# Attention feeding a soft mixture of experts: x transposed in its own cycle, logits and slot sums one pair sooner, one group left at the end

## The chip, the cores and the metric

The kernel runs on one core of a Trainium2 chip, as one program. The time is device microseconds of one execution; of several executions the median is given. A profile of one further execution gives the rows below.

## The reference, cut to what matters

Three stages follow each other: attention inside chunks of 64 positions, a soft mixture of experts over the resulting 4608 x 512 matrix `x`, and a gated feed-forward layer.

```python
# attention, B=8, H=8, S=576, D=64, chunks of 64
scores = scale * (q_c @ k_c.T); scores -= scores.max(-1)
attn = exp(scores); attn /= attn.sum(-1) + 1e-9
x = (attn @ v_c) -> 4608 x 512
# mixture: N=4608 tokens, 8 experts x 4 slots = 32 slots
logits = x @ phi
d = exp(logits - logits.max(0)); d /= d.sum(0) + 1e-9
slot_input = d.T @ x                       # 32 x 512
for e in range(8):                          # w1: 512 x 1024, w2: 1024 x 512
    slot_out[e] = relu(slot_input[e] @ w1[e]) @ w2[e]
c = softmax over the slots of logits
x = c @ slot_out
# gated layer, d_ff = 1536
out = (silu(x @ w_gate) * (x @ w_val)) @ w_out
```

The weights of the gated layer arrive as 64-bit floats and are turned into single precision on the chip; the experts' weights are single precision.

## The kernel before, in words

The order of the instructions on each engine is the order in which the code is written.

**The attention loop.** It takes 36 tiles of 128 tokens, two at a time: 18 pairs. Iteration `k` does, on TensorE (PE): for the pair `a = k - 1` the product with v (`emit_pv`, tiles `xa_ps`, `xb_ps`); then either the logits of a group of four tiles (`emit_logits`, `lt_ps`) or the slot sums of a group (`emit_si`, `si_ps`); then the transposes of the exponentials' input for pair `k` (`emit_pt`, `pt_ps`), the scores of pair `k + 1` (`emit_scores`, `s_ps`), the transposes of `x` (`emit_xt`, `xt_ps`), and after logits the transpose of their exponentials (`emit_et`, `e_ps`). The logits run over all tokens, so the maximum per slot is a running one, and `acc` (slot sums) and `zst` (denominators) are rescaled by `beta_t` group by group.

**Who evacuates.** VectorE (DVE) takes the scores' maximum and subtracts it (`m`, `ssb`, lines 336 and 338), makes `x` out of `xa_ps` and `xb_ps` (`rec`, `x_sb`, lines 381 to 388), the running maximum (`mx`, `mn`) and `acc`. ScalarE (ACT) takes the exponentials (`pt`, `et`), copies `xt` and keeps a copy of the logits in `lt_all`. The PSUM pool `ps_t` has three buffers that `lt`, `pt`, `xt`, `e`, `si` take in turn: the first `xt_ps` of an iteration with logits gets the buffer of `lt_ps`, and so waits for `lt_all` (line 453).

**Loads.** All come from the queue of SyncE (SP), in the order of the code. `load_qk` follows the scores of the tile that had the buffer (four buffers), `load_v` follows its product (four buffers). `pump(1)` at the end of an iteration takes the next load from a list `lq` into one of 16 slots of 1 MB (`wp`): pieces of w1 and w2 in the main. Iterations with `k % 4 == 3` take none, except that the sixteenth takes two. Behind the loop four more slots (`wx`) open in the memory of the q, k and v buffers; from there on a piece is requested when a slot is freed, and the first are freed by the first products with w1 (`emit_w1`, `h_ps`).

**Conversion steps on the side.** From `k = 4` on `conv_step` puts one step of a weight's conversion at an iteration's end: step a (lines 185 to 187) at `k` = 4 and 7, b (194, 195) at 5 and 8, c (200) at 6 and 9.

**The tail and the experts.** Behind the loop two groups of logits (7 and 8) and two of slot sums remain. Then `sips` (line 623) forms the slots' inputs, and the experts run: `emit_w1` for six experts, `emit_w2` for two, and so on by the list `order`. The gated layer follows.

Of the kernel before, what the change touches and what calls it, by code (L numbers as in the profile page):

```python
# [8 lines left out]
F32 = mybir.dt.float32  # L9
# [24 lines left out]
def tile_attn_softmoe_swiglu(  # L34
# [12 lines left out]
    nc = tc.nc  # L47
# [220 lines left out]
    with tc.manual_schedule():  # L268
# [126 lines left out]
        def emit_xt(i):  # L395
            xt = xtp.tile([128, 4, 128], F32, tag="xt", name="xt")
            n = 4 if i < NTILE - 1 else 2
            for j0 in range(0, 4, n):
                ps = ps_t.tile([128, 4, 128], F32, tag="t", name="xt_ps")
                for j in range(j0, j0 + n):  # L400
                    nc.tensor.transpose(ps[:, j - j0, :], x_t[i][:, j * 128:(j + 1) * 128], ident)  # L401
                if j0 == 0:
                    nc.scalar.activation(out=xt[:, 0:n], in_=ps[:, 0:n], func=ACTF.Copy)  # L403
                else:
                    nc.vector.tensor_copy(out=xt[:, j0:j0 + n], in_=ps[:, 0:n])
            xt_t[i] = xt
# [4 lines left out]
        lt_t = {}  # L411
        lx_t = {}

        def emit_lmm(g, lt=None):
            if lt is None:
                lt = ps_t.tile([128, 512], F32, tag="t", name="lt_ps")
            lt_t[g] = lt
            for kk in range(4):
                for jt in range(4):
                    nc.tensor.matmul(  # L420
                        out=lt[32 * jt:32 * jt + 32, 0:128],
                        lhsT=phi_sb[:, kk, :],
                        rhs=xt_t[4 * g + jt][:, kk, :],
                        start=(kk == 0), stop=(kk == 3),
                        tile_position=(0, 32 * jt),
                    )

        def emit_lmax(g):
            lt = lt_t[g]
            mx = sm.tile([128, 1], F32, tag="mx", name="mx")  # L430
            mn = sm.tile([128, 1], F32, tag="mn", name="mn")
            nc.vector.tensor_reduce(out=mx, in_=lt[:, 0:128], axis=AX.X, op=ALU.max)
            if g:
                nc.vector.tensor_scalar(out=mn, in0=mx, scalar1=mrun[0], scalar2=-1.0, op0=ALU.max, op1=ALU.mult)
            else:
                nc.vector.tensor_scalar(out=mn, in0=mx, scalar1=-1.0, scalar2=None, op0=ALU.mult)
            if g:
                nc.vector.tensor_tensor(out=mx, in0=mx, in1=mrun[0], op=ALU.max)
            lx_t[g] = mn, mrun[0]
            mrun[0] = mx  # L440
# [15 lines left out]
        def emit_logits(g):  # L456
            emit_lmm(g)
            emit_lmax(g)
            emit_lexp(g)
# [3 lines left out]
        def emit_et(g, sums=True):  # L463
            et, z = et_t[g]
            ps = ps_t.tile([128, 512], F32, tag="t", name="e_ps")
            nc.tensor.transpose(ps[:, 0:128], et, ident)
            e = atp.tile([128, 128], F32, tag="e", name="e", bufs=1)
            nc.scalar.activation(out=e, in_=ps[:, 0:128], func=ACTF.Copy)
            e_t[g] = e
            if sums:  # L470
                emit_zst(g)

        def emit_zst(g):
            z = et_t.pop(g)[1]
            if g:
                nc.vector.scalar_tensor_tensor(out=zst, in0=zst, scalar=beta_t[g], in1=z, op0=ALU.mult, op1=ALU.add)
            else:
                nc.vector.tensor_copy(out=zst, in_=z)

        def emit_si(g):  # L480
            e = e_t.pop(g)
            ps = ps_t.tile([128, 512], F32, tag="t", name="si_ps")
            for jt in range(4):
                nc.tensor.matmul(  # L484
                    out=ps[32 * jt:32 * jt + 32, :],
                    lhsT=e[:, 32 * jt:32 * jt + 32],
                    rhs=x_t.pop(4 * g + jt),
                    start=True, stop=True,
                    tile_position=(0, 32 * jt),
                )  # L490
            if g:
                be = beta_t.pop(g)
                n = DM // 2 if g == NG - 1 else DM
                for o in range(0, DM, n):
                    nc.vector.scalar_tensor_tensor(
                        out=acc[:, o:o + n], in0=acc[:, o:o + n], scalar=be, in1=ps[:, o:o + n],
                        op0=ALU.mult, op1=ALU.add,
                    )
            else:
                nc.vector.tensor_copy(out=acc, in_=ps)  # L500
# [3 lines left out]
        def emit_m1():  # L504
            mps = ps_t.tile([128, 512], F32, tag="t", name="mps")
            nc.tensor.transpose(mps[0:1, 0:128], mrun[0], ident)
            nmrow = sm.tile([1, 4, 32], F32, tag="nmrow", name="nmrow", bufs=1)
            nc.vector.tensor_reduce(
                out=nmrow[:, 0, :], in_=mps[0:1, 0:128].rearrange("p (j s) -> p s j", s=32), axis=AX.X, op=ALU.max,
                negate=True,  # L510
            )
            for jj in range(1, 4):
                nc.vector.tensor_copy(out=nmrow[:, jj, :], in_=nmrow[:, 0, :])
            tail['nmrow'] = nmrow

        def emit_m2():
# [28 lines left out]
        for k in range(NP + 1):  # L545
            a = k - 1
            if a >= 0:
                emit_pv(a)
            if k == NP:
                break  # L550
            if a >= 3 and a % 2:
                emit_logits((a - 3) // 2)
            elif a >= 4:
                emit_si((a - 4) // 2)
            emit_pt(2 * k)
            emit_pt(2 * k + 1)
            if k + 1 < NP:
                emit_scores(k + 1)
                spread_v(2 * k + 2)
                spread_v(2 * k + 3)  # L560
            if a >= 1:
                emit_xt(2 * a - 2)
                emit_xt(2 * a - 1)
            if a >= 3 and a % 2:
                emit_et((a - 3) // 2)
            if k == 0 or k % 4 != 3:
                pump(1)
            elif k + 1 == NP - 2:
                pump(2)
            conv_step(k >= 4 and conv_pos() < 2 and not conv_busy())  # L570
# [3 lines left out]
        auto[0] = True  # L574
        pump()
        g = NG - 1
        lt2 = ps_s.tile([128, 2, 512], F32, tag="s", name="lt_ps")
        emit_xt(NTILE - 4)
        emit_xt(NTILE - 3)
        emit_lmm(g - 1, lt2[:, 0])  # L580
        emit_xt(NTILE - 2)
        emit_lmax(g - 1)
        emit_xt(NTILE - 1)
        emit_lexp(g - 1)
        emit_lmm(g, lt2[:, 1])
        emit_et(g - 1, False)
        emit_lmax(g)
        emit_lexp(g)
        emit_zst(g - 1)
        emit_m1()  # L590
        emit_si(g - 1)
        emit_et(g, False)
        emit_m2()
        nc.scalar.activation(out=lt_all[:, g, :], in_=lt_t[g][:, 0:128], func=ACTF.Copy)
# [1 line left out]
        emit_zst(g)  # L596
        emit_si(g)
        conv_until(2)
        warm(3)
        p1.close()  # L600

        p2 = ctx.enter_context(tc.tile_pool(name="p2", bufs=1))
# [416 lines left out]
```

## Time and profile before

| what | value |
|---|---|
| median of 3 runs | 545.47 us (544.68 to 545.85) |
| the profiled execution's own time | 543.5 us |
| its span, first to last instruction | 541.7 us |
| mean granted TensorE clock | 0.996 of full speed |
| PE busy over the span | 521.3 us (96%) |
| DVE, ACT, POOL busy | 406.7, 260.4, 252.9 us |
| attention with its tail | to about 130 us |
| experts | about 131 to 169 us |
| gated layer | the rest |

The span is 1.8 us under the execution's time, and that time is 2.0 us under the median of the runs. Busy time of PE is not work at its peak: matmuls wait inside the pipeline too, and their ends are modelled.

### The profile page before, as it was taken

Reading aid. Unit: us, or ns where it says so; the run is one execution under the profiler, and the core shown is the slowest. Engines: PE = TensorE matmul, PEld = TensorE weight load, DVE = VectorE, ACT = ScalarE, POOL = GpSimd, SP = SyncE. Lnnn points to the kernel's source line nnn. Section 1 sums busy time; section 2 is a strip of 40 time slices with the busy share of each in tenths; the row PEclk is TensorE's granted clock in tenths of the full one; section 3 lists DMA queues with packets and bytes.
Section 4 is the critical chain, followed back from the end, with each engine's and each line's share of the span. In section 5 each row is a group of like instructions: output and inputs, shape, how many; then the busy total and the mean of one; then the engine's idle time right before and its main releaser. Section 6 shows DMA issues by size and latency. Waiting matters only on the chain.

```text
span 541.7 us, 11039 instructions
## 1 busy us (share of the span) xinstructions
PE 521.3 (96%) x4389; PEld 409.8 (76%) x4389; DVE 406.7 (75%) x673; ACT 260.4 (48%) x504; POOL 252.9 (47%) x252
## 2 busy tenths in 40 slices
PE   7899999998998889999999999999999999999997
PEld 6778887873335568888888888888888888888885
DVE  5778987864766999888898889989898943433554
ACT  1344533342447766666565555545654533333331
POOL 3333343321002576576566756656664743343342
PEclk9999999999999989999999999999999999999999
DMA  8999999999999502020202220222000000222344
GB/s 324 404 358 398 348 405 347 413 416 400 421 416 417 247 1 77 2 78 2 77 1 77 77 79 0 79 79 77 0 1 0 3 0 1 77 79 77 113 179 174
DMA packets 23762, 91.09 MB, mean 168 GB/s; under 512 B 3104, under 2 KB 3104, under 8 KB 17696
## 3 DMA queue, kind: packets, MB, share of 16 engines
q1 hardware_dynamic: 23712, 90.40, 43.1%
q8 instruction: 34, 0.56, 0.4%
q14 instruction: 16, 0.13, 0.1%
HBM read 80.95 MB, written 9.44 MB: 167 GB/s over the span
## 4 chain that ended last, share of the span: by engine, by line
PE 81%; DVE 9%; DMA 6%; issue 2%; ACT 1%; POOL 0%; SPq 0%; ACTq 0%; DVEq 0%
PE o L891 18%; PE o L893 18%; PE o L892 18%; DMA w2t<-in_moe_w_dram 6%; PE v_ps L847 4%; PE g_ps L847 4%; PE xa_ps L365 4%; PE xt_ps L401 3%; PE s_ps L328 3%; PE pt_ps L351 2%; PE gg_ps L828 2%; PE si_ps L484 1%; DVE ssb L338 1%; DVE m L336 1%; PE h_ps L652 1%
## 5 line engine op out<-in xcount | busy, mean ns | idle before, releaser
L860 POOL TENSOR_TENSOR lo_sb<-s_sb,hi_sb 128x512 fp32r<-128x512 f32 x106 | 140.5, 1326 | 130.9 <-ACT hi_sb L859 127.9
L891 PE MATMUL o<-whl,hi_sb 128*128 128x512 f32 x428 | 167.7, 392 | 2.5 <-DVE part L900 2.5
L893 PE MATMUL o<-whl,lo_sb 128*128 128x512 f32 x428 | 167.2, 391 | 0.5 <-POOL lo_sb L860 0.5
L892 PE MATMUL o<-whl,hi_sb 128*128 128x512 f32 x428 | 167.1, 390 | 0.0
L850 ACT ACTIVATE s_sb<-g_ps 128x512 f32<-128x512 f32 (+1 forms) x110 | 64.7, 590 | 149.9 <-PE g_ps L847 147.7
L851 DVE TENSOR_TENSOR s_sb<-s_sb,v_ps 128x512 f32<-128x512 f32 (+1 forms) x110 | 74.0, 674 | 74.5 <-ACT s_sb L850 73.2
L891 PEld LDWEIGHTS o<-whl,hi_sb 128*128 128x128 f32 x428 | 80.6, 188 | 22.2 <-DVE part L900 4.5
L893 PEld LDWEIGHTS o<-whl,lo_sb 128*128 128x128 f32 x428 | 80.6, 188 | 17.8 <-POOL lo_sb L860 0.9
L892 PEld LDWEIGHTS o<-whl,hi_sb 128*128 128x128 f32 x428 | 80.6, 188 | 16.3
L859 ACT ACTIVATE hi_sb<-s_sb 128x512 fp32r<-128x512 f32 (+1 forms) x110 | 67.6, 616 | 0.8 <-DVE s_sb L851 0.8
L904 DVE TENSOR_TENSOR part<-part,o 128x512 f32<-128x512 f32 x92 | 57.1, 677 | 2.6 <-PE o L893 2.6
L318 POOL COPY vbd<-vbd 64x520 f32<-64x520 f32 x36 | 22.3, 619 | 69.9 <-DMA vbd<-in_v_dram 56.2
L213 POOL TENSOR_TENSOR mt<-mt,ex 128x512 f32<-128x512 f32 x32 | 39.5, 1234 | 27.5 <-PE g_ps L847 13.8
L200 DVE SCALAR_TENSOR_TENSOR ex<-raw,ex 128x512 uint16<-128x512 uint16 x32 | 47.2, 1477 | 0.1
L847 PE MATMUL v_ps<-c_t,g_st 128*128 128x512 f32 (+1 forms) x110 | 42.5, 390 | 0.8 <-DMA raw<-in_moe_w_val_dram 0.5
L847 PE MATMUL g_ps<-c_t,g_st 128*128 128x512 f32 (+1 forms) x110 | 42.4, 389 | 0.1
L353 ACT ACTIVATE pt<-pt_ps 128x512 f32<-128x512 f32 x36 | 19.5, 596 | 36.2 <-PE pt_ps L351 36.2
L195 DVE SCALAR_TENSOR_TENSOR mt<-mt,raw 128x512 f32<-128x512 f32 x32 | 34.9, 1090 | 0.0
L336 DVE TENSOR_REDUCE m<-s_ps 128x16 f32<-128x1024 f32 x18 | 22.0, 1224 | 14.8 <-PE s_ps L328 14.7
L187 DVE TENSOR_SCALAR mt<-raw 128x512 int32<-128x512 int32 x32 | 32.9, 1027 | 0.0
L365 PE MATMUL xa_ps<-vbd,pt 128*64 128x130 f32 x432 | 28.2, 277 | 0.0
L403 ACT ACTIVATE xt<-xt_ps 128x512 f32<-128x512 f32 (+1 forms) x36 | 19.3, 596 | 13.7 <-PE xt_ps L401 10.2
(138 smaller groups left out, 664.2 us busy)
## 6 DMA issues: line engine op xcount, KB each, us to landing
qk<-in_qk_dram SPq DMA_DIRECT2D x36, 512.0 KB, 6.6
w1t<-in_moe_w_dram SPq DMA_DIRECT2D x16, 1024.0 KB, 9.3
w2t<-in_moe_w_dram SPq DMA_DIRECT2D x15, 1024.0 KB, 13.5
vbd<-in_v_dram SPq DMA_DIRECT2D x36, 260.0 KB, 7.5
out_dram<-part SPq DMA_DIRECT2D x36, 256.0 KB, 2.2
raw<-in_moe_w_out_dram SPq DMA_DIRECT2D x6, 1024.0 KB, 7.1
raw<-in_moe_w_gate_dram SPq DMA_DIRECT2D x5, 1024.0 KB, 4.8
raw<-in_moe_w_val_dram SPq DMA_DIRECT2D x5, 1024.0 KB, 5.1
```

Source lines behind the costliest of these rows:

```text
L200: nc.vector.scalar_tensor_tensor(out=ex, in0=hh, scalar=0x8000, in1=ex, op0=ALU.bitwise_and, op1=ALU.bitwise_or)
L213: nc.gpsimd.tensor_tensor(out=m, in0=m, in1=p, op=ALU.mult)
L365: nc.tensor.matmul(out=banks[n // 3][64 * cc:64 * cc + 64, (n % 3) * 2 * VW:(n % 3 + 1) * 2 * VW], lhsT=pt_t[i][:, j, 64 * cc:64 * cc + 64 ...
L847: nc.tensor.matmul(out=ps[:, k], lhsT=g_st[:, c, gi, ff:ff + 128], rhs=c_blk(b)[:, k], start=True, stop=True)
L850: nc.scalar.activation(out=s[:, k], in_=gp[:, k], func=ACTF.Silu)
L851: nc.vector.tensor_tensor(out=s[:, k], in0=s[:, k], in1=vp[:, k], op=ALU.mult)
L859: nc.scalar.activation(out=hi[:, k], in_=s[:, k], func=ACTF.Copy)
L860: eng.tensor_tensor(out=lo[:, k], in0=s[:, k], in1=hi[:, k].bitcast(F32), op=ALU.subtract)
L891: nc.tensor.matmul(out=a, lhsT=hi[:, ts], rhs=w_hi, start=first, stop=False)
L892: nc.tensor.matmul(out=a, lhsT=hi[:, ts], rhs=w_lo, start=False, stop=False)
L893: nc.tensor.matmul(out=a, lhsT=lo[:, ts], rhs=w_hi, start=False, stop=last)
L904: nc.vector.tensor_tensor(out=p[:, t], in0=p[:, t], in1=a, op=ALU.add)
```

## The change

`x` of pair `a` is transposed at the end of the iteration that makes it, not one iteration later. Logits of a group follow in the iteration after its second pair's (`a` even instead of odd), and its slot sums one iteration sooner too (`a` odd). So one group of logits and two of slot sums remain behind the loop, not two and two; the tail's second PSUM tile goes, and so do three small matmuls on the identity (`warm(3)`). Three copies of a row become one copy with a broadcast input. The calls of `pump` stay where they were.

```diff
-        def emit_lmm(g, lt=None):
-            if lt is None:
-                lt = ps_t.tile([128, 512], F32, tag="t", name="lt_ps")
-            lt_t[g] = lt
+        def emit_lmm(g):
+            lt = lt_t[g] = ps_t.tile([128, 512], F32, tag="t", name="lt_ps")
...
-            for jj in range(1, 4):
-                nc.vector.tensor_copy(out=nmrow[:, jj, :], in_=nmrow[:, 0, :])
+            nc.vector.tensor_copy(out=nmrow[:, 1:4, :], in_=nmrow[:, 0:1, :].to_broadcast([1, 3, 32]))
...
-            if a >= 3 and a % 2:
-                emit_logits((a - 3) // 2)
-            elif a >= 4:
-                emit_si((a - 4) // 2)
+            if a >= 2 and a % 2 == 0:
+                emit_logits((a - 2) // 2)
+            elif a >= 3:
+                emit_si((a - 3) // 2)
             emit_pt(2 * k)
             emit_pt(2 * k + 1)
             if k + 1 < NP:
                 emit_scores(k + 1)
...
-            if a >= 1:
-                emit_xt(2 * a - 2)
-                emit_xt(2 * a - 1)
-            if a >= 3 and a % 2:
-                emit_et((a - 3) // 2)
+            if a >= 0:
+                emit_xt(2 * a)
+                emit_xt(2 * a + 1)
+            if a >= 2 and a % 2 == 0:
+                emit_et((a - 2) // 2)
...
         g = NG - 1
-        lt2 = ps_s.tile([128, 2, 512], F32, tag="s", name="lt_ps")
-        emit_xt(NTILE - 4)
-        emit_xt(NTILE - 3)
-        emit_lmm(g - 1, lt2[:, 0])
+        emit_si(g - 1)
         emit_xt(NTILE - 2)
-        emit_lmax(g - 1)
         emit_xt(NTILE - 1)
-        emit_lexp(g - 1)
-        emit_lmm(g, lt2[:, 1])
-        emit_et(g - 1, False)
+        emit_lmm(g)
         emit_lmax(g)
         emit_lexp(g)
-        emit_zst(g - 1)
         emit_m1()
-        emit_si(g - 1)
         emit_et(g, False)
...
         conv_until(2)
-        warm(3)
```

On PE, at the start of the loop (iterations 1 to 3: product with v, transposes `pt_ps`, scores), the order before is this:

```order
L365 MATMUL xb_ps<-vbd_102,pt 64x130 x4
L351 MATMUL pt_ps<-ident,ssb 128x128 x8
L328 MATMUL s_ps<-qk_97 64x64 x16
L328 MATMUL s_ps<-qk_98 64x64 x16
L365 MATMUL xa_ps<-vbd_103,pt 64x130 x8
L365 MATMUL xa_ps<-vbd_104,pt 64x130 x4
L365 MATMUL xb_ps<-vbd_104,pt 64x130 x4
L351 MATMUL pt_ps<-ident,ssb 128x128 x8
L328 MATMUL s_ps<-qk_99 64x64 x16
L328 MATMUL s_ps<-qk_100 64x64 x16
L401 MATMUL xt_ps<-ident,x_sb 128x128 x8
```

The same place with the change:

```order
L365 MATMUL xb_ps<-vbd_102,pt 64x130 x4
L351 MATMUL pt_ps<-ident,ssb 128x128 x8
L328 MATMUL s_ps<-qk_97 64x64 x16
L328 MATMUL s_ps<-qk_98 64x64 x16
L401 MATMUL xt_ps<-ident,x_sb 128x128 x8
L365 MATMUL xa_ps<-vbd_103,pt 64x130 x8
L365 MATMUL xa_ps<-vbd_104,pt 64x130 x4
L365 MATMUL xb_ps<-vbd_104,pt 64x130 x4
L351 MATMUL pt_ps<-ident,ssb 128x128 x8
L328 MATMUL s_ps<-qk_99 64x64 x16
L328 MATMUL s_ps<-qk_100 64x64 x16
L401 MATMUL xt_ps<-ident,x_sb 128x128 x8
```

Eight transposes of `x` now stand between the scores of iteration 1 and the next product with v, where there were none.

On PE, in the tail from the last transposes of `x` to the first product with w1, before:

```order
L420 MATMUL lt_ps<-xt,phi_sb 32x128 x16
L401 MATMUL xt_ps<-ident,x_sb 128x128 x8
L420 MATMUL lt_ps<-xt,phi_sb 32x128 x16
L466 MATMUL e_ps<-ident,et 128x128
L506 MATMUL mps<-ident,mx 1x128
L484 MATMUL si_ps<-x_sb,e 32x512 x4
L466 MATMUL e_ps<-ident,et 128x128
L518 MATMUL nps<-ident,nmrow 128x1
L484 MATMUL si_ps<-x_sb,e 32x512 x4
L536 MATMUL warm<-ident 128x128 x3
L623 MATMUL sips<-rsel,acc 128x32 x4
L652 MATMUL h_ps<-w1t,si_m 32x512 x8
```

With the change:

```order
L482 MATMUL si_ps<-x_sb,e 32x512 x4
L401 MATMUL xt_ps<-ident,x_sb 128x128 x8
L418 MATMUL lt_ps<-xt,phi_sb 32x128 x16
L504 MATMUL mps<-ident,mx 1x128
L464 MATMUL e_ps<-ident,et 128x128
L515 MATMUL nps<-ident,nmrow 128x1
L482 MATMUL si_ps<-x_sb,e 32x512 x4
L611 MATMUL sips<-rsel,acc 128x32 x4
L640 MATMUL h_ps<-w1t,si_m 32x512 x8
```

One set of logits, eight transposes of `x` and the three `warm` matmuls have left the tail.

## Rows read from the trace of the kernel before

**Rows 1.** Chain that ended last, 130 to 235 us: start, duration, what

```profile
138.05 15.14 DMA w2t<-in_moe_w_dram
153.21 15.51 DMA w2t<-in_moe_w_dram
```

**Rows 2.** Stretches: length, busy PE, PEld, DVE, ACT, POOL, clock, DMA share, GB/s

```profile
34.00:42.00 8.00, 8.00 (x158) 6.35 (x158) 7.31 (x13) 4.50 (x10) 2.43 (x5) 1.00 0.91 331
...
84.00:93.00 9.00, 9.00 (x206) 7.34 (x207) 6.69 (x12) 5.11 (x13) 4.46 (x8) 1.00 0.91 322
93.00:132.00 39.00, 36.13 (x617) 26.69 (x617) 25.38 (x65) 14.70 (x43) 10.66 (x22) 1.00 1.02 414
132.00:134.00 2.00, 2.00 (x23) 0.67 (x19) 0.98 (x5) 0.06 (x1) 0.11 (x1) 1.00 0.93 315
134.00:168.00 34.00, 34.00 (x292) 12.72 (x284) 22.78 (x89) 16.96 (x35) 2.31 (x8) 1.00 1.01 418
```

**Rows 3.** Timeline of SP, requests: start, duration, what

```profile
84.76 1.10 SPq L285 DMA_DIRECT2D qk<-in_qk_dram  x2
...
131.88 9.04 SPq L89 DMA_DIRECT2D w2t<-in_moe_w_dram  x9
```

**Rows 4.** Chain, 84 to 130 us: an iteration with slot sums, one with logits

```profile
86.19 0.11 PE e_ps L466
86.30 1.48 PE xa_ps L365 x24
87.78 0.44 PE xb_ps L365 x8
88.22 0.99 PE si_ps L484 x8
89.22 1.03 PE pt_ps L351 x8
90.24 1.09 PE s_ps L328 x64
91.33 1.02 PE xt_ps L401 x8
92.36 1.48 PE xa_ps L365 x24
...
97.51 1.14 PE xt_ps L401 x8
...
98.81 1.48 PE xa_ps L365 x24
```

**Rows 5.** Timeline of PE, iterations 1 to 3; in brackets idle time before

```profile
13.89 1.06 PE L351 MATMUL pt_ps<-ident,ssb 128*128 128x128 f32 x8 [0.77 <-DVE rec L382]
...
18.74 1.09 PE L351 MATMUL pt_ps<-ident,ssb 128*128 128x128 f32 x8 [0.68 <-DVE ssb L338]
...
21.37 0.50 PE L328 MATMUL s_ps<-qk 64*64 64x64 f32 x18 [0.69 <-issue]
...
27.60 0.33 PE L328 MATMUL s_ps<-qk 64*64 64x64 f32 x3 [0.68 <-issue]
```

**Rows 6.** Timeline of DVE: conversion step a, an evacuation behind it; one behind slot sums

```profile
36.95 0.66 DVE L186 TENSOR_SCALAR tmp<-raw 128x512 uint16<-128x512 uint16 x1
37.52 0.83 DVE L187 TENSOR_SCALAR tmp<-raw 128x512 int32<-128x512 int32 x1
38.27 0.15 DVE L381 TENSOR_SCALAR rec<-xa_ps 128x12 f32<-128x12 f32 x1
...
51.18 0.96 DVE L384 TENSOR_TENSOR x_sb<-xa_ps,rec 128x768 f32<-128x768 f32 x1 [0.53 <-PE si_ps L484]
```

**Rows 7.** Timeline of PE, the first products with w1

```profile
130.76 1.92 PE L652 MATMUL h_ps<-w1t,si_m 128*32 128x512 f32 x16 [0.34 <-DVE si_m L630]
```

**Rows 8.** Stretches in the tail and behind the experts, columns as in rows 2

```profile
120.00:131.00 11.00, 8.64 (x111) 5.14 (x111) 5.77 (x25) 4.19 (x15) 1.74 (x6) 1.00 1.01 416
190.00:192.00 2.00, 0.00 (x0) 0.00 (x0) 2.00 (x3) 1.06 (x2) 2.00 (x2) 1.00 0.00 0
192.00:194.00 2.00, 1.86 (x5) 1.48 (x6) 2.00 (x5) 0.00 (x0) 0.65 (x2) 0.59 0.00 0
```

## The prediction

> **What bounds the kernel now.** I read three views. First the chain that ended last, to see on what the stage of the experts ends: two pieces of it, 15.14 and 15.51 us, are the arrival of w2 [rows 1]. From 138 us to 168.7 us nothing that PE does matters; the stream of weights sets the end, and the gated layer follows it stiffly. Second, the busy time in stretches, with the rate of the DMA engines. From 134 to 168 us they move 418 GB/s, and 414 from 93 to 132 us; but 331 and 322 in two stretches of the attention loop, and 315 for two microseconds at 132 [rows 2]. So the stream is nearly always full, and has a few thin places. The reader is to see in them that an earlier request can gain time only while the stream is thin: at a thin place the DMA engines have run down their requests and wait for the kernel. Behind the last thin place of the loop (84 to 93 us) the stream is full up to the tail's. Hence my model: the end of the experts moves by as much as the requests around 84 to 93 us move, plus or minus what happens at 132 us. Third, the chain and the timelines of PE and DVE, to see who sets those requests. In the loop they follow PE: q and k are asked for when a tile's scores are done, v behind the product. The request at 84.76 us belongs to the scores of iteration 12 [rows 3].
>
> **A full iteration on PE.** With slot sums it runs from 86.30 to 92.36 us, 6.06 us; its pieces are 1.48 + 0.44 + 0.99 + 1.03 + 1.09 + 1.02 = 6.05 [rows 4]. PE waits for nothing there. With logits it runs from 92.36 to 98.81 us, 6.45 us. The difference lies ahead of the transposes of x: the product ends at 94.28 (92.36 + 1.48 + 0.44), the transposes start at 97.51, 3.23 us later, and they wait for the copy of the logits that frees their buffer [rows 4]. The change keeps the order of the three buffers (logits or slot sums, two of `pt`, two of `xt`, `e`), so an iteration with logits still has this wait, and one with slot sums still has none. In the steady loop I cost the change at nothing. The new need, that x of this pair be ready for its own transposes, is covered: PE does slot sums or logits, `pt` and scores in between (0.99 + 1.03 + 1.09 = 3.11), and the wait of x for the slot sums (0.53, [rows 6]) goes, since the buffer of x is freed an iteration sooner.
>
> **What is added ahead of iteration 12's requests.** Work that used to lie behind is done sooner. Up to the scores of iteration 12 PE does one more set of transposes of x (1.02, pair 0 in iteration 1), one more of slot sums (0.99) and one more transpose of exponentials (0.11): 2.12 us [rows 4]. The number of logits up to there is five in both. SP's queue has the same order, so nothing is moved past a load; but each load is issued when PE is there, so this work makes requests later, not sooner.
>
> **What swallows it.** PE idles early. In iterations 1 and 2 it waits 0.77 and 0.68 us for VectorE ahead of `pt` [rows 5]. The transposes of pair 0 come behind the first of these and ahead of the second: 0.68 is swallowed, 0.34 left. Then there are two waits of 0.69 and 0.68 us put down to "issue", in the middle of scores, behind 46 and 61 of their 64 matmuls [rows 5]; no tile ends there. By the emitted order 127 matmuls lie between the two, and they end 6.23 us apart while the stream is full; later, where PE takes as long for as much, such waits of this size are not in the loop. I read them as tied to time rather than to work: whatever PE waits for comes at its own pace, and a PE that gets there later waits less. Then the first takes the 0.34 that is left, and the second 0.68 of the rest. Swallowed: 0.68 + 0.34 + 0.68 = 1.70. Bounds: 0.68, if the two waits stay as they are in spite of more work ahead of them; all 2.12, if the iteration's other gaps take the rest.
>
> **What the new parity costs.** Step a of a conversion ends iteration 4, and takes DVE from 36.95 to 38.27 us, just ahead of the evacuation of x [rows 6]. Now the iteration behind it has slot sums, and PE does not feel it. With the change that iteration has logits, and their chain (x, maximum, exponentials, copy, buffer) has no slack: the 3.23 us above already exceed PE's own work in between. I take +0.6 for it, half of the step and nearest to what sticks out past the product with v. Bounds: 0, and the whole step, 1.32. Steps b and c keep company with logits half of the time in either version, and I cost them at nothing; their cover is the slack of iterations with slot sums.
>
> So requests around 84 to 93 us come 2.12 - 1.70 + 0.6 = 1.0 us later.
>
> **The tail.** The thin place at 132 us costs 2 x (418 - 315)/418 = 0.5 us [rows 2]. It is there because the first slots are freed by w1's products, which start at 130.76 us [rows 7], and the next request goes out at 131.88 us [rows 3], when the stream has nearly run dry. With the change the tail loses eight transposes of x (1.02) and a set of logits with its waits, while the loop ends about 1.0 later: w1 starts no later than now, and the stream, itself 1.0 later, still has work when the request comes. The 0.5 is given back. Bounds: 0 to 0.5, no more. That the tail gets shorter by still more buys nothing: PE would wait for w2 longer. The `warm` matmuls and the two saved copies lie off the path of the stream: nothing, as long as w2 is what the experts wait for.
>
> **Sum.** +1.0 - 0.5 = +0.5 us, against the profiled execution's 543.5 us (span 541.7) 544.0 us. The median of the runs lies 2.0 us above that execution; I add the same difference to it: 545.47 + 0.5 = 546.0 us. About 0.2%, 1.1 us, is what a measurement of this kernel tells from no change; this is inside.
>
> **A rule against the trace.** The two thin stretches move 331 and 322 GB/s, the full one 418 [rows 2]. The Trainium skill (DMA: Bandwidth & Descriptors, Specifications) names some 358 GB/s as the limit from HBM for a core. By it the thin stretches would be nearly full, requests would not count, and the sum would be 0, 545.5 us. The trace disagrees: 418 GB/s over 34 us.
>
> **Rivals.**
> - *Nothing swallowed* (slower). If the two "issue" waits stay and step a costs all of its 1.32, requests come 2.12 - 0.68 + 1.32 = 2.8 later: with the tail's 0.5 back 545.47 + 2.3 = 547.8 us. For it: waits that belong to a place in the program move with it. Against: both stand where the stream is fullest, and more work ahead of them should shrink them. It decides from a shift of 1.6 us at iteration 12. Chance 0.21, with the halves of it that end at 547.
> - *DVE's wait was on the path* (faster). The 0.53 us behind slot sums goes four times before iteration 12, 2.1 us; if PE gets its `ssb` sooner by that, 546.0 - 2.1 = 543.9 us. For it: between 34 and 42 us DVE is busy 7.31 of 8 us [rows 2]. Against: the iteration with slot sums has 0.01 us to give [rows 4]. Chance 0.11.
> - *The clock falls in the tail* (slower). Behind 2 us with no matmul at all the granted clock read 0.59, a mix of 2.4 and 1.2 GHz; in the tail, with PE busy 8.64 of 11 us, it stayed 1.00 [rows 8]. Without `warm`, between the last slot sums and `sips`, there is about a microsecond of idle. At 1.2 GHz w1's first group of 1.92 us [rows 7] would take up to 3.8, the first requests come 1 us later, the 0.5 is not given back and about as much is added: 547.0 us. The Trainium skill (TensorE: Matmul & The Clock Gate, What's actually happening) has the throttled clock as the default that only activity lifts, which speaks for this rival; the tail's 1.00 speaks against it here. Chance 0.03.
> - *The change does nothing to the stream*: 545.5 us, inside the forecast's class.
>
> **How the numbers follow.** The forecast (a change within 0.2%, 545.0 to 546.5 by itself) has 0.65, and holds the last rival. Slower takes 0.21 + 0.03 = 0.24, faster 0.11. The range goes from 544.2, which leaves out most of the faster rival, to 547.6, which leaves out the outer part of the slower ones: about 2 in 10 outside.
>
> **What the new profile would show.** Step by step: transposes of x behind the scores at about 16 us, and the wait ahead of the next `pt` gone; the two "issue" waits shorter; the transposes of x behind logits at about 42 us late by half a microsecond or more; q and k of iteration 12 asked for at about 85.8 us; a thin stretch at 84 to 94 us, none at 132 us; w1's products at about 130 us; the last w2 at about 169.2 us. The prediction is wrong if that last arrival moves by more than 1.1 us, above all if the thin stretches of the loop fill up, or if the gated layer behind does not follow stiffly.

## The result, and the profile after

| what | before | with the change |
|---|---|---|
| median | 544.61 us (8 runs, 543.67 to 546.15) | 548.45 us (8 runs, 546.12 to 549.79) |
| ratio | | 1.0065, 95% interval 1.0044 to 1.0087 |
| profiled execution, span | 541.7 us | 545.1 us |
| first `sot_ps` after the experts | 170.07 us | 173.41 us |
| first product with w1 | 130.76 us | 132.86 us |

The change makes the kernel slower, by 3.5 us by the ratio. The spans differ by 3.4 us, and 3.34 of that is there when the experts end; so the loss is in the attention, its tail or the experts, and the gated layer follows stiffly: it is as long as before, only later. The two profiled executions took 543.5 and 546.9 us, 1.1 and 1.6 us less than the medians of their kernels.

The shares of the chain that ended last, with the change (page, first line of part 4):

```profile
PE 88%; DVE 6%; issue 2%; POOL 1%; ACT 1%; DMA 1%; SPq 0%; ACTq 0%; DVEq 0%; POOLq 0%
```

The two pieces of w2, 15.14 and 15.51 us [rows 1], are gone. The chain of the changed kernel through the experts (start, duration, what) is PE's work:

```profile
132.86 3.64 PE h_ps L640 x16
...
167.04 5.07 PE so_ps L683 x46
...
173.41 1.17 PE sot_ps L774 x8
```

The first piece answers to [rows 7]: 1.92 us before, 3.64 now, for the same 16 matmuls. The stretches of the changed kernel say why (columns as in rows 2):

```profile
34.00:42.00 8.00, 7.09 (x185) 6.11 (x176) 7.20 (x14) 3.23 (x10) 2.44 (x5) 1.00 0.87 298
...
84.00:93.00 9.00, 8.90 (x225) 7.30 (x218) 7.08 (x15) 3.16 (x9) 4.46 (x8) 1.00 0.89 320
...
126.00:128.00 2.00, 1.06 (x20) 0.53 (x10) 0.85 (x4) 0.64 (x3) 1.21 (x4) 1.00 1.04 426
128.00:130.00 2.00, 1.61 (x11) 0.45 (x10) 0.85 (x5) 0.73 (x3) 0.32 (x2) 0.89 1.00 410
130.00:132.00 2.00, 1.42 (x9) 1.39 (x7) 0.87 (x2) 0.00 (x0) 0.00 (x0) 0.50 1.01 418
132.00:134.00 2.00, 1.67 (x11) 0.79 (x14) 0.48 (x5) 0.28 (x1) 0.20 (x1) 0.50 0.91 377
134.00:136.00 2.00, 2.00 (x12) 0.20 (x4) 0.00 (x0) 0.00 (x0) 0.00 (x0) 0.50 0.48 143
136.00:138.00 2.00, 2.00 (x19) 0.78 (x19) 0.98 (x5) 0.18 (x1) 0.11 (x1) 0.91 0.85 295
```

Against [rows 2] the reader is to see two things. In the tail the granted clock is 0.50, which is 1.2 GHz, from 130 to 136 us, where it was 1.00 before; and the thin place of the stream, 315 GB/s at 132 us before, is now 143 GB/s at 134 us. The requests of SP (columns as in rows 3) show the place of both ends:

```profile
86.30 0.81 SPq L285 DMA_DIRECT2D qk<-in_qk_dram  x2
...
134.86 9.89 SPq L89 DMA_DIRECT2D w2t<-in_moe_w_dram  x9
```

Iteration 12 asks 1.54 us later than before, the first freed slot is asked for 2.98 us later [rows 3]. PE's timeline of the changed kernel shows the waits (idle time before in brackets):

```profile
19.09 1.09 PE L351 MATMUL pt_ps<-ident,ssb 128*128 128x128 f32 x8
...
21.33 0.58 PE L328 MATMUL s_ps<-qk 64*64 64x64 f32 x25 [0.41 <-issue]
...
35.48 1.55 PE L365 MATMUL xa_ps<-vbd,pt 128*64 128x130 f32 x24
...
41.52 1.14 PE L401 MATMUL xt_ps<-ident,x_sb 128*128 128x128 f32 x8 [0.91 <-ACT lt_all L451]
...
42.75 1.55 PE L365 MATMUL xa_ps<-vbd,pt 128*64 128x130 f32 x24
...
82.77 0.27 PE L365 MATMUL xa_ps<-vbd,pt 128*64 128x130 f32 x1 [0.68 <-issue]
...
107.11 0.38 PE L401 MATMUL xt_ps<-ident,x_sb 128*128 128x128 f32 x2 [0.81 <-DVE m L336]
...
119.01 1.14 PE L401 MATMUL xt_ps<-ident,x_sb 128*128 128x128 f32 x8 [1.18 <-ACT lt_all L451]
...
120.25 1.55 PE L365 MATMUL xa_ps<-vbd,pt 128*64 128x130 f32 x24
...
127.50 0.27 PE L504 MATMUL mps<-ident,mx 128*1 128x128 f32 x1 [0.92 <-DVE mx L436]
...
130.61 1.92 PE L611 MATMUL sips<-rsel,acc 128*128 128x32 f32 x8 [0.58 <-DVE acc L493]
```

At the last transposes of `x` in the loop, ahead of the last product with v, the kernel before waited less:

```profile
115.84 1.15 PE L401 MATMUL xt_ps<-ident,x_sb 128*128 128x128 f32 x8 [0.31 <-ACT pt L353]
```

**The balance.** The profiled execution divides at the last product with v, the 18th (120.25 us here, 116.9 before), and at the first product with w1. The loop up to there is 3.3 us later; the way from there to w1 takes 12.6 instead of 13.8 us, 1.2 less; from w1 to `sot_ps` it is 40.55 (173.41 - 132.86) instead of 39.31 us (170.07 - 130.76), 1.24 more. 3.3 - 1.2 + 1.24 = 3.34 us.

**Where the loop is later.** The fifth product with v starts at 35.5 us in both profiles; behind it the loop takes 3.4 us longer. Of this 0.7 us lies in the fifth and sixth steps (from product to product), 1.8 us in the two pairs of steps with the waits at 82.77 and 107.11 us, and 1.0 us in the last step: it takes 6.66 instead of 5.68 us, because the set of logits that left the tail now stands there in place of slot sums, with its wait of 1.18 us. The loop holds eight sets of logits where it held seven. The profiles of the runs described below show the same shift: from the first to the last product with v the old order takes 104.5 to 107.0 us in five profiles (before, e3, e7, e8, e14), the new one 108.3 to 110.1 us in nine (changed kernel, e1, e2, e4, e5, e6, e9, e13, e15).

### The profile page after: what moved, and what is told of

It is laid out like the page before. It is cut to its first block, busy times and chain, and to the rows that moved or that the text cites. A ratio compares the mean times of both kernels' runs of the same rounds, so it can differ in the third digit from the quotient of the medians.

```text
span 545.1 us, 11019 instructions
## 1 busy us (share of the span) xinstructions
PE 522.5 (96%) x4383; PEld 409.6 (75%) x4383; DVE 405.8 (74%) x671; ACT 260.0 (48%) x504; POOL 252.8 (46%) x252
## 4 chain that ended last, share of the span: by engine, by line
PE 88%; DVE 6%; issue 2%; POOL 1%; ACT 1%; DMA 1%; SPq 0%; ACTq 0%; DVEq 0%; POOLq 0%
PE o L879 17%; PE o L881 17%; PE o L880 17%; PE xa_ps L365 5%; PE v_ps L835 4%; PE g_ps L835 4%; PE xt_ps L401 3%; PE s_ps L328 3%; PE h_ps L640 3%; PE pt_ps L351 3%; PE so_ps L683 3%; PE gg_ps L816 2%; PE si_ps L482 1%; PE xb_ps L365 1%; PE lt_ps L418 1%
## 5 line engine op out<-in xcount | busy, mean ns | idle before, releaser
L213 POOL TENSOR_TENSOR mt<-mt,ex 128x512 f32<-128x512 f32 x32 | 39.5, 1233 | 26.7 <-PE g_ps L835 13.8
L365 PEld LDWEIGHTS xa_ps<-vbd,pt 128*64 128x64 f32 x432 | 23.7, 135 | 3.8 <-issue 2.6
```

What stands on the lines that cost most here:

```text
L213: nc.gpsimd.tensor_tensor(out=m, in0=m, in1=p, op=ALU.mult)
L365: nc.tensor.matmul(out=banks[n // 3][64 * cc:64 * cc + 64, (n % 3) * 2 * VW:(n % 3 + 1) * 2 * VW], lhsT=pt_t[i][:, j, 64 * cc:64 * cc + 64 ...
```

## The experiments

Every time is a median of 12 executions (6 for e10, e11 and e12), with the ratio to before on the same chip. A profile shows one execution: those of e3, e4, e8 and e12 are the slowest of their runs, and that of e13 the second slowest. Where a kernel adds matmuls on the identity, nobody reads their result; no run leaves out any of the work.

| run | median us | before us | ratio, 95% |
|---|---|---|---|
| e1_warm_back | 546.28 | 544.67 | 1.0039, 1.0015 to 1.0063 |
| e2_fill | 545.84 | 544.67 | 1.0026, 1.0002 to 1.0049 |
| e3_before_nowarm | 546.61 | 544.67 | 1.0046, 1.0021 to 1.0071 |
| e4_after_again | 548.03 | 544.67 | 1.0055, 1.0032 to 1.0077 |
| e5_lt_own | 545.45 | 544.43 | 1.0007, 0.9988 to 1.0026 |
| e6_pump_all | 546.61 | 544.43 | 1.0022, 1.0004 to 1.0041 |
| e7_before_fill | 545.23 | 544.43 | 1.0014, 0.9993 to 1.0036 |
| e8_before_warm10 | 546.59 | 544.43 | 1.0037, 1.0018 to 1.0056 |
| e9_conv5 | 544.77 | 544.48 | 1.0003, 0.9984 to 1.0021 |
| e10_pad | 548.91 | 544.48 | 1.0077, 1.0055 to 1.0098 |
| e11_xt_four | 548.72 | 544.48 | 1.0075, 1.0056 to 1.0095 |
| e12_xt_four_conv5 | 548.67 | 544.48 | 1.0078, 1.0054 to 1.0101 |
| e13_after_conv5 | 547.67 | 544.83 | 1.0045, 1.0019 to 1.0071 |
| e14_before_conv5 | 546.73 | 544.83 | 1.0018, 0.9998 to 1.0039 |
| e15_lt_own_conv5 | 546.18 | 544.83 | 1.0016, 0.9998 to 1.0035 |

### The clock in the tail: e1 to e4

e1 puts `warm(3)` back into the changed kernel, e3 takes it out of the kernel before, e4 is the changed kernel once more.

```diff
         conv_until(2)
+        warm(3)
         p1.close()
```

> The changed kernel with the three matmuls on the identity put back between the last slot sums and the slots' inputs, nothing else. Clock theory (the granted clock is at half from 129.8 to 136.5 us because PE does less behind the loop; it costs 1.7 us on w1's first group and 0.9 us on the slots' inputs): the clock stays at 1.00 up to w1, w1's first group takes 1.9 and not 3.6 us, and the time falls by 2 to 2.6 us from the changed kernel's. Loop theory (the last product with v starts 3.3 us later than before, and w1 starts 2.1 later for it): no change within 0.5 us, as the matmuls stand behind the loop.

> The kernel before without its three matmuls on the identity ahead of the slots' inputs. Clock theory in its narrow form (it is these three that held the clock): half clock from about 128 us on, 2 to 2.6 us slower than before. Clock theory in its wide form (the shorter tail has less matmul work in all: one set of logits and eight transposes are gone too): within 0.5 us of before. Loop theory: no change.

> The changed kernel unchanged, on the same chip, for a second trace. Clock theory: the half clock in the tail again, at about the same place, w1's first group near 3.6 us, 3 to 4 us over before. Loop theory: the two waits put down to issue in the loop (0.68 at 82 us, 0.81 at 106 us) again, the last product with v 3 us later than before. If the half clock is missing here and the time is the same 3.5 us over, the clock theory falls.

e2 puts matmuls on the identity into four gaps of the changed tail, in a buffer of the scores (`fill(n)`, as `warm` but with its own tile).

```diff
         emit_si(g - 1)
+        fill(2)
...
         emit_lmm(g)
+        fill(3)
         emit_lmax(g)
...
         emit_et(g, False)
+        fill(1)
...
         conv_until(2)
+        fill(3)
```

> The changed kernel with matmuls on the identity in each of the tail's idle stretches (2 ahead of the last transposes of x, 3 behind the last logits, 1 ahead of the row's transpose, 3 ahead of the slots' inputs). Clock theory: no half clock in the tail, w1's first group 1.9 us, the thin stretch of the stream at 133 to 140 us shrinks to what it was before (0.5 us lost), and the time is 2.5 us under the changed kernel's, within 1 us of the kernel before. Loop theory: the clock may stay up, but the time stays within 1 us of the changed kernel's, 3 us over the kernel before.

e2's tail keeps the full clock, and its first products with w1 take what they took before. Stretches and PE's timeline of e2:

```profile
132.00:134.00 2.00, 1.66 (x16) 0.97 (x19) 0.48 (x5) 0.28 (x1) 0.20 (x1) 1.00 1.03 426
134.00:136.00 2.00, 2.00 (x23) 0.73 (x19) 0.70 (x5) 0.00 (x0) 0.11 (x1) 1.00 0.84 320
```

```profile
133.13 1.92 PE L650 MATMUL h_ps<-w1t,si_m 128*32 128x512 f32 x16 [0.34 <-DVE si_m L628]
```

The old kernel without its three `warm` matmuls, e3, shows a loss by itself. Its stretches, from an execution of 552.17 us, 5.6 over its median:

```profile
128.00:130.00 2.00, 1.24 (x18) 0.46 (x14) 1.05 (x5) 0.92 (x4) 1.45 (x5) 0.81 0.98 406
130.00:132.00 2.00, 2.00 (x10) 0.28 (x2) 0.72 (x5) 0.00 (x0) 0.08 (x1) 0.50 1.05 414
...
136.00:138.00 2.00, 1.66 (x9) 1.00 (x12) 0.48 (x5) 0.28 (x1) 0.20 (x1) 0.50 0.21 86
138.00:140.00 2.00, 2.00 (x16) 0.39 (x8) 0.00 (x0) 0.00 (x0) 0.00 (x0) 0.50 0.00 0
```

What follows. The fall of the clock is a cause: filling the gaps gives 2.2 us back (548.03 to 545.84; by the ratios 0.29%, 1.6 us), and taking `warm` out of the old kernel costs 1.9 us with nothing else changed. In the profiles `sips` takes 1.92 us in the changed kernel and 1.08 in e2, and w1's first group 3.64 and 1.92: at half clock these two are 2.6 us longer. With w1 at half clock the first slots come free late, and the stream runs dry while PE is slow (0 GB/s at 138 us in e3). In e1 the clock still read 0.50 at 130 to 132 us, against what was expected, but 0.76 at 132 to 134, and w1's first group took 1.92 us again: in this execution the three matmuls, just ahead of `sips`, brought the clock back in time for w1 and did not prevent its fall. Against e4's twelve executions, e2's mean is 2.0 us lower (95% interval 0.8 to 3.2) and e1's 1.4 lower (-0.1 to 2.9), so e1 alone doesn't show a gain. The Trainium skill (TensorE: Matmul & The Clock Gate, What's actually happening) has the throttled clock as the default that only activity lifts; the trace of e1 agrees, with 0.50 at 130 to 132 us, when the three matmuls begin, and 1.00 from 134 us on.

How much of the loss against before is the clock's is not settled, because the old tail falls too (e14 and e8 below). Over whole executions the granted clock averages 0.9947 in the kernel before (115 executions) and 0.9933 in the changed one (20, e4 among them); an estimate from this difference is 0.8 us of 545. And five of these 20 executions read 0.997: they still take 546.1 to 548.9 us, where the 52 of before at 0.996 or more take 544.3 in the median. In e2, with the tail at full clock, the way from the last product with v to w1 is 11.96 us, 1.9 less than the 13.84 before. That is less than the 3 us by which the new loop is longer, and the difference, some 1.3 us, is about what e2 stands over before (0.26%, 1.4 us).

### The requests of the loop: e6

e6 is e2 with a piece requested in every iteration.

```diff
-            if k == 0 or k % 4 != 3:
-                pump(1)
-            elif k + 1 == NP - 2:
-                pump(2)
+            pump(2 if k + 1 == NP - 2 else 1)
```

> The kernel of e2 with a request for an expert's piece at the end of every iteration, so that the thin stretches of the loop have work. Theory of the prediction (the end follows the last thin place of the loop): the stretches at 34 to 42, 59 to 70 and 84 to 93 us fill up to 400 GB/s, and the time falls by 1.5 to 2.5 us. Theory that the end follows the first products with w1: the stream only runs dry sooner in the tail, as no more than 20 pieces have room; no change within 0.7 us, or slower by up to 1 us if q and v arrive late behind the pieces.

Its stretches (the same as in rows 2, and two of the tail):

```profile
34.00:42.00 8.00, 7.69 (x200) 6.68 (x191) 6.56 (x13) 3.79 (x11) 2.61 (x5) 1.00 1.02 406
...
84.00:93.00 9.00, 8.90 (x225) 7.63 (x221) 7.21 (x14) 3.55 (x10) 3.94 (x7) 1.00 1.02 405
132.00:134.00 2.00, 1.67 (x17) 0.96 (x20) 0.48 (x5) 0.28 (x1) 0.20 (x1) 1.00 0.15 61
134.00:136.00 2.00, 2.00 (x23) 0.74 (x19) 0.73 (x5) 0.00 (x0) 0.11 (x1) 1.00 0.39 78
```

The thin places of the loop are full, the pieces come earlier, and the kernel gains nothing: 0.22% over before, where e2 stood 0.26% over it. The stream merely runs out of free slots sooner, 61 and 78 GB/s at 132 to 136 us. So the end of the experts does not move with the requests of the loop. From the first product with w1 to `sot_ps` it is 38.82 or 38.83 us in the profiles of e1, e5 to e9, e11, e12, e14 and e15, however early the pieces came (e6: 171.94 - 133.11 = 38.83): PE's own work. Before it was 39.31, and in e2 too, each with a wait for w2 at the end; so w2 was late by only 0.49 us there (0.78 in e10). e7 shows what follows: its w1 starts 0.85 us later than before's (131.61), and its `sot_ps` only 0.36 later (170.43).

### Step a of the conversion: e9, e13, e14

e9 is e2, e13 the changed kernel without a fill and e14 the kernel before, each with the first conversion one iteration later.

```diff
-            conv_step(k >= 4 and conv_pos() < 2 and not conv_busy())
+            conv_step(k >= 5 and conv_pos() < 2 and not conv_busy())
```

> The kernel of e2 with the conversion steps begun one iteration later (from iteration 5 on), so that the first step a lies ahead of an iteration with slot sums and not one with logits. If step a ahead of logits is what makes the stretch from the fifth to the sixth product with v 7.1 to 7.3 us instead of 6.1: that stretch falls to 6.5, w1 starts 0.5 us sooner or so, and the time falls by as much. If not: the stretch stays above 7.

> The changed kernel with the first conversion step at iteration 5 rather than 4, and nothing that fills the tail. If step a ahead of logits and the clock's fall in the tail are two separate losses, the 5th step of the loop (product to product) falls from about 7.1 to 6.45 us and the median to 1.0 to 1.3 us under the changed kernel's 548.0 to 548.5, so 546.8 to 547.4, and the tail still shows a stretch at a granted clock of 0.50 to 0.9. If the step was nothing by itself and only the fill helped: 548 or more. If the clock's fall comes from where the loop stands in time: no stretch under 0.95, and 545 us.

> The kernel before with the first conversion step at iteration 5 rather than 4, so that step a stands ahead of an iteration with logits, as in the changed kernel. If the parity is what costs: the step behind it grows from 6.45 to about 7.1 us, and the median is 0.6 to 1.3 us above before's on the same chip. If a conversion one iteration later is simply better: no change or 0.3 to 1 us faster.

PE's timeline of e9 at the iteration that stood 0.91 us for `lt_all` in the changed kernel:

```profile
35.85 1.55 PE L365 MATMUL xa_ps<-vbd,pt 128*64 128x130 f32 x24
...
41.06 1.14 PE L401 MATMUL xt_ps<-ident,x_sb 128*128 128x128 f32 x8
...
42.30 1.55 PE L365 MATMUL xa_ps<-vbd,pt 128*64 128x130 f32 x24
```

Product to product it takes 6.45 instead of 7.27 us (42.75 - 35.48; in e2 it is 7.17), 0.7 to 0.8 less, as in e13 (6.45). With the fill, that brings the kernel to before's time: 1.0003. But the shares can't be told apart by the medians: the intervals of e9 and e2 overlap, and e13 (1.0045) lies only 0.1% under e4 (1.0055), its clock in the tail still 0.50.

e14 has step a ahead of logits in the old order, and there the transposes of `x` waited 0.31 us for `lt_all`, and product to product took 6.65 us, like the other iterations with logits. So the place alone doesn't make the loss: the 7.1 us that were expected did not come. The step is also shorter there. DVE and POOL in the changed kernel, then DVE in e14:

```profile
36.71 0.62 POOL L318 COPY vbd<-vbd 64x520 f32<-64x520 f32 x1
36.99 0.62 DVE L186 TENSOR_SCALAR tmp<-raw 128x512 uint16<-128x512 uint16 x1
37.39 0.69 POOL L319 MEMSET vbd<- 64x520 f32 x1
37.53 0.83 DVE L187 TENSOR_SCALAR tmp<-raw 128x512 int32<-128x512 int32 x1
```

```profile
42.72 0.42 DVE L186 TENSOR_SCALAR tmp<-raw 128x512 uint16<-128x512 uint16 x1
43.05 0.42 DVE L187 TENSOR_SCALAR tmp<-raw 128x512 int32<-128x512 int32 x1
```

At 37 us POOL spreads v at the same time, and the two operations take 0.62 and 0.83 us; at 42.7 us it does not, and they take 0.42 each. The delay was the step at its long size ahead of logits. e6 shows it in the new order, with step a at its old place: POOL did not work beside it there, and the transposes of `x` waited 0.31 instead of 0.91 us. DVE and PE in e6:

```profile
37.15 0.42 DVE L186 TENSOR_SCALAR tmp<-raw 128x512 uint16<-128x512 uint16 x1
37.48 0.42 DVE L187 TENSOR_SCALAR tmp<-raw 128x512 int32<-128x512 int32 x1
```

```profile
41.06 1.14 PE L401 MATMUL xt_ps<-ident,x_sb 128*128 128x128 f32 x8 [0.31 <-ACT lt_all L451]
```

Product to product it took 6.66 us there. e14's median is 1.9 us above before all the same, though its ratio can't be told from no change (0.9998 to 1.0039), and its profile has the half clock in the tail (0.58 at 126 to 128 us, 0.50 to 132 us, 12 GB/s at 134 us) although `warm(3)` is there: the old tail is not safe from it either.

### The waits put down to issue: e10

e10 is e2 with ten more matmuls on the identity ahead of the loop, `warm(14)` for `warm(4)` behind the first scores. A matmul of `warm` leaves two records, so PE has 20 more.

> The kernel of e2 with ten more matmuls on the identity (20 in the trace) behind the first scores, in PE's idle time there. If the waits put down to issue belong to places in the program (they lie 126 to 127 matmuls of the trace apart, or a multiple of it): they come 20 matmuls earlier, in iteration 2 behind 19 of the 64 matmuls of the scores and not 39, in iteration 12 behind 2 of the product's matmuls and not 22, in iteration 15 in the scores' end and not in the transposes. If they belong to tiles or to time: they stay where they were. The time: within 0.7 us of e2 either way.

In the changed kernel, e1, e2, e4, e6 and e15 the wait of iteration 12 stands behind 22 of the 24 matmuls of `xa_ps`, with 0.39 to 1.21 us. In e10 it stands behind 3, 19 sooner. PE's timeline of e10, from there on:

```profile
81.93 1.43 PE L365 MATMUL xa_ps<-vbd,pt 128*64 128x130 f32 x21 [0.48 <-issue]
...
94.83 1.06 PE L401 MATMUL xt_ps<-ident,x_sb 128*128 128x128 f32 x8 [1.83 <-DVE m L336]
95.73 0.27 PE L464 MATMUL e_ps<-ident,et 128*128 128x128 f32 x1
95.93 1.55 PE L365 MATMUL xa_ps<-vbd,pt 128*64 128x130 f32 x24
97.31 0.61 PE L365 MATMUL xb_ps<-vbd,pt 128*64 128x130 f32 x8
97.86 1.06 PE L482 MATMUL si_ps<-x_sb,e 128*32 128x512 f32 x8
98.85 1.09 PE L351 MATMUL pt_ps<-ident,ssb 128*128 128x128 f32 x8
99.88 1.16 PE L328 MATMUL s_ps<-qk 64*64 64x64 f32 x64
100.97 0.66 PE L401 MATMUL xt_ps<-ident,x_sb 128*128 128x128 f32 x4
102.13 0.60 PE L401 MATMUL xt_ps<-ident,x_sb 128*128 128x128 f32 x4 [0.50 <-issue]
...
109.11 0.45 PE L328 MATMUL s_ps<-qk 64*64 64x64 f32 x13 [1.47 <-issue]
```

Between the wait at 94.83 and that at 102.13 lie 8 + 1 + 24 + 8 + 8 + 8 + 64 + 4 = 125 recorded matmuls, and a few records can be missing. In the changed kernel the wait of iteration 15 stood behind 6 of 8 transposes of `x` (107.11 us, put down to DVE, though `x` was ready); in e10 it stands behind 51 of the 64 scores ahead of them, again 19 sooner. So these waits belong to places in PE's stream of instructions, some 126 matmuls apart, and not to data or to the time. They come at some of the places, with 0.2 to 1.9 us, and their sizes differ from execution to execution. The one of iteration 15 stands in eleven profiles of the new order, with 0.8 to 1.9 us (changed kernel, e1, e2, e4 to e6, e9, e10, e12, e13, e15). e10 loses 3.1 us against e2, where 0.7 at most was expected, with its clock at 1.00 in the tail. Its profile shows the loop as the main place: 111.5 us from the first to the last product with v, 110.1 in e2, of the 2.3 us between the spans.

What PE waits for there, and why some places cost nothing, no run shows. There is a candidate: the changed kernel's profile page counts 34 packets on a queue of instructions (`q8 instruction: 34, 0.56, 0.4%`), and 4383 matmuls with as many weight loads on PE. If that queue feeds PE, this makes 129 matmuls for each packet, an estimate near the 126, and PE would be waiting for the next part of its own program. No run changes those packets, so this stays untested.

### Other repairs: e5, e7, e8, e11, e12, e15

e5 is e2 with the logits of the last group inside the loop in a buffer of the scores, so that no transpose waits for their copy (1.18 us at 119.01 in the changed kernel); in its profile the second half of these transposes waits 1.24 us for `pt` instead. e7 fills the old tail's gaps with two more `warm(3)`, e8 has `warm(10)` for `warm(3)` in the old kernel. e11 is e5 with `x` of two pairs transposed together in the iterations with slot sums, e12 is e11 with the conversion from iteration 5, e15 is e5 with the same.

```diff
-            lt = lt_t[g] = ps_t.tile([128, 512], F32, tag="t", name="lt_ps")
+            if g == NG - 2:
+                lt = ps_s.tile([128, 2, 512], F32, tag="s", name="lt_ps")[:, 0]
+            else:
+                lt = ps_t.tile([128, 512], F32, tag="t", name="lt_ps")
+            lt_t[g] = lt
```

```diff
-            if a >= 0:
+            if a % 2 and a >= 1:
+                for i in range(2 * a - 2, 2 * a + 2):
+                    emit_xt(i)
+            elif k == NP - 1:
                 emit_xt(2 * a)
```

> The kernel of e2 (the changed kernel with the tail's idle stretches filled), with the logits of group 7 in the scores' buffer instead of the shared three, so that the last iteration's transposes of x do not wait for the copy of the logits (1.18 us in the changed kernel's trace). Theory that the end follows the first products with w1 (the first slots are freed there, and the stream is dry by then): w1 starts about 1 us sooner than in e2, and the time falls by about 1 us, to the kernel before's. Theory of the prediction (the end follows the requests around 84 to 93 us): no change, as this lies behind them.

> The kernel before with matmuls on the identity in its tail's idle stretches (3 ahead of the last logits, 3 ahead of the row of maxima). Clock theory: the clock never falls in the tail, so the slower of the runs go and the median falls by 0.3 to 0.7 us; if the fall behind the loop was rare in the kernel before, no change. Either way a second trace of the old loop: the theory that the new loop is 3 us longer wants its first to last product with v at 106 to 107 us, the theory that loops differ that much from run to run wants 108 or more in one of them.

> The kernel before with ten matmuls on the identity ahead of the slots' inputs instead of three: PE is kept busy, and w1 starts about 1.7 to 2.0 us later, nothing else moves. Theory that the end follows the first products with w1: 1.5 to 2 us slower. Theory that the stream has slack at that place: 0 to 0.5 us slower.

> The kernel of e5 with the transposes of x of two pairs together in each iteration with slot sums, and none in those with logits (but the last). Theory that the end follows w1's start, and that the new loop is long by early transposes and by the wait of the transposes behind logits: the loop from the first to the last product with v takes 106 us or less and not 109, w1 starts 2 to 3 us sooner than in e2, and the time falls by 2 to 3 us, 1 to 2 under the kernel before's. Theory of the prediction (requests at 84 to 93 us): these come sooner as well, so faster too, but by no more than 1 us. If four evacuations in a row on ScalarE hold PE up, the iteration with slot sums takes over 7.6 us, and nothing is gained.

> The kernel of e11 with the conversion steps begun at iteration 5. With e9's step a: up to 0.5 us under e11; if DVE has room ahead of logits in the new order: the same as e11 within 0.5 us.

> The changed kernel with the tail filled, group 7's logits in a buffer of the scores and the first conversion step at iteration 5: all three repairs together. If each repair gives what it gave alone (2.2, 1.1 and 0.4 us of the loss of 3.4 to 3.9): within 0.5 us of before, 544.2 to 545.0. If the order of the change itself is better once its side costs are gone: below 543.9. If the waits put down to issue decide: 545.5 to 547, with 1 us or more of them in the profile.

e5 can't be told from before, nor from e2, and e7 can't be told from before. e7's clock averages 0.9974 over its executions, against 0.9944 before on the same chip, and still nothing is gained; whether the added matmuls cost what the clock gives back, no run shows. e8 is slower by 0.37%; its profile has the clock below 1.00 at 128 to 133 us in spite of ten `warm` matmuls. e11, expected to gain 2 to 3 us over e2, and e12 lose 0.75 and 0.78% against before. Their loops are more regular where no wait falls (6.97 and 5.75 us in turn), but e12's profile has five waits put down to issue of 0.87 to 1.89 us in the loop, 5.67 together, and a clock of 0.96 from 93 to 132 us; e11's has 0.98 and 0.86, and 1.34 put down to ACT, too little for its median, so that the cause of e11's loss is not settled. e15 takes three repairs together and stands at 1.0016, no better than e5 or e9 with two: they don't add up. Its profile has waits of 0.77 and 0.82 us put down to issue, and 1.58 us at the place in iteration 15. No version here beats the kernel before.

## Why the prediction was wrong, step by step

The forecast was 546.0 us, a change within 0.2%, in a range of 544.2 to 547.6; 548.45 us was measured, 0.65% slower.

- **"From 138 us to 168.7 us nothing that PE does matters"**: wrong, and the first step that failed. The chain names what came last, not by how much: PE was busy 34.00 of 34.00 us there in [rows 2], and w2 was late by 0.49 us only. A shift of w1 by more than that goes through, as e7 shows. e6 shows the other half: requests in the loop, made early, gain nothing.
- **Swallowed, 1.70 of 2.12 us**: early in the loop even more was swallowed. The fifth product starts at 35.5 us in both kernels, so all 2.12 were, the upper bound; the second wait of [rows 5] for `ssb` is gone. But that the two waits put down to issue shrank was luck: they are not "tied to time", e10 moved them by moving instructions. Waits of their kind come later, 0.68 at 82.77 and 0.81 at 107.11 us, where the loop before had one of 0.25 (at 83.09). The rival *Nothing swallowed* had them as places in the program, which e10 bears out; its 2.8 us at iteration 12 did not come.
- **Step a, +0.6**: right in size, steps 5 and 6 of the loop together take 13.33 instead of 12.65 us, +0.7; e6, with the short step, takes 12.72. Its mechanism is the one given, with the addition that the step was long because POOL worked beside it.
- **Requests of iteration 12, +1.0**: +1.54, 86.30 for 84.76. The product of iteration 12 starts 0.96 us later (80.54 for 79.58), 0.7 of it by step a; behind it comes the wait of 0.68 at 82.77 instead of the 0.25. The sum left out that one more iteration with logits, 6.45 us instead of 6.06, lies ahead of that product in the new order.
- **The tail, "w1 starts no later than now" and 0.5 given back**: wrong. The loop did not end "about 1.0 later" but 3.3: what was added was summed up to iteration 12 only, and the set of logits whose loss shortens the tail came into the loop's last step, with its wait. w1 starts 2.1 us later, the thin place got deeper, and w1's first group took 3.64 us.
- **`warm` "off the path of the stream: nothing"**: the term put at nothing that cost most by a run of its own. By e3 the three matmuls are worth 1.9 us in the old kernel, and filling gives back 1.6 to 2.2 us in the new one. The rival *The clock falls in the tail* had the mechanism, and was given 0.03. It took the 1.00 of the old tail [rows 8] as evidence that the clock holds, but that tail had the `warm` matmuls in it and no idle stretch just ahead of `sips`.
- **The sum.** With the tail filled the change is worth +0.26% (e2, 0.02 to 0.49%), 1.4 us, where the sum had +0.5; the sign was right, and the size too small. With the clock's fall it is +3 to 3.5.

Settled: the fall of the clock costs time in both kernels, and filling gives back 1.6 to 2.2 us in the changed one. Step a is 0.7 to 0.8 us in the profiles, not separable in the medians. The rest goes with a loop that is longer by more than the tail is shorter; the waits at places of the instruction stream are part of it, and no run here controls their sizes. How the 3.5 us divide among these three is open.

## What to carry to other kernels

When the chain ends on a transfer, look how busy the engine beside it is before calling its work free: one that is busy all the time is the next bound, and the slack between the two is the number to work with. Small matmuls on the identity in front of a group of dependent steps can be worth more than the work that a change saves (here three were worth 1.9 us); take them away in an experiment of their own, and don't expect more of them to help more (e8). And if an order of instructions moves waits that belong to the stream of instructions, single profiles mislead: compare medians of a dozen executions.

## What was not expected of the hardware

- PE waits at places of its own instruction stream, some 126 recorded matmuls apart, for 0.2 to 1.9 us; adding 20 records ahead of the loop moved them by 19.
- The granted clock fell to 0.50 in a tail in which PE was busy 1.06 of 2 us (126 to 128 us) and 1.61 of 2 us (128 to 130 us), with no wait over 0.92 us. In the old tail PE was busy 0.93 of 2 us at 122 to 124 us, and the clock stayed 1.00; in e14 the same tail fell (0.58 at 126 to 128 us). In these profiles the busy share alone doesn't tell which.
- Two DVE operations of 128x512 took 0.42 us each alone, 0.62 and 0.83 beside POOL's copies and memsets (changed kernel); in all seventeen profiles the second took 0.83 to 0.85 us where a memset ran beside it, and 0.42 where only a copy did or nothing.
